# Another written order of issue in a packed attention and gated convolution kernel on one core

## The chip, the core and the metric

One core of a Trainium2 chip runs the whole kernel. TensorE (PE), VectorE (DVE), ScalarE (ACT) and GpSimd (POOL) each take their instructions strictly in the order in which the program lists them; SyncE (SP) only issues the transfers. The metric is the device time in microseconds (us) of one execution; for a kernel it is the median of its runs.

## What is computed

Per batch (8 of them) and head (8 heads, 576 rows, 64 columns), 32 packed queries `p` attend to `k` and `v`; the 576 queries `q` then attend to the 32 packed rows. The heads side by side give `x` (576 x 512), which goes through a causal convolution over 5 rows with a sigmoid, and through two 512 x 512 products:

```python
p_packed = sm_attn(p, k, v)
x = sm_attn(q, p_packed, p_packed)
gate = sigmoid(sum(conv_w[t] * shifted(x, 4 - t) for t in range(5)))
out = (gate * (x @ w_val)) @ w_out
```

The three weights arrive as 64-bit floats and are rebuilt on the chip from their two 32-bit words.

## The kernel before, in words

The work of a batch is cut into pieces, and each kind of piece is a Python generator that issues one piece at every step. A letter names the generator and a digit the batch: `K`, `V`, `Q`, `P` and `L` issue the loads of k, v, q, p and of the weights; `W`, `C` and `O` rebuild w_val, conv_w and w_out; `k` and `q` transpose keys and queries on PE; `a` is the packed attention, `p` transposes its result, `s` and `t` are the second attention's scores and weights, `w` the product of the packed rows with w_val, `x` the second attention's output, `g` the convolution and gate, `v` the value product, `o` the product with w_out and the store. The string `ORDER` (lines 46 to 79) lists the steps one by one; `K0.2` is two steps of `K0`. `run` (line 608) goes through it, and the class `InOrder` (line 82) chains every instruction to the one before it on its engine, so that the string is the order of issue of all five engines. Almost everything has line 90 in the profile for that reason, and groups are told apart by their tiles.

```python
for token in order.split():
    what, n = (token + ".1").split(".")[:2]
    ...
    for _ in range(int(n)):
        next(gens[what])
```

What matters for the steps that follow:

- `load` (line 191) brings a half batch of k, v or q in one transfer, into one of two buffers of its kind (`km`, `vm`, `qm`). `load_p` (185) brings p twice over. `words_of` (208) brings the words of a quarter of w_val in two transfers and of w_out in one, into five buffers.
- `transposed` (302) makes `kpt` or `qpt` on PE (three times 4 transposes a half batch), which ACT copies to `kT` or `qT`. `turned` (324) does the same with p (`pTt`, `pT`) and with the packed result (`ppTt`, `ppT`).
- `attn_pack` (340): scores `s`, their maximum `nb` on DVE, the exponential `a` on ACT, three transposes `at` on PE copied to `a1t` by ACT, the product `pv` with v, scaled to `ppd`.
- `attn_out` (388) and `weighted` (413): scores `s`, a transpose `t` and a maximum `mx` on DVE, a subtraction on POOL, an exponential on ACT, a sum and a reciprocal on DVE, a product on POOL, a transpose `a` on DVE, its rounded and rest parts `a2h` (ACT) and `a2l` (DVE).
- `packed_values` (442): `wp` on PE, split into `wph` (ACT) and `wpl` (DVE). `mixed` (457): `x` on PE, copied to `xp` by ACT. `value` (509): `val` on PE, twelve matmuls; DVE multiplies it into `sig`, ACT and DVE split that into `gvh` and `gvl`. `project` (562): `o` on PE, twelve matmuls for a chunk of 128 rows.
- `gate` (489): ACT starts an accumulator `sig` with the first tap, and DVE adds the other four, each one reading what the one before it wrote.
- `scores`, `packed_values`, `mixed` and the packed product `pv` use parts of PE's array: their matmuls take 64 rows by 32 columns (`s`, `wp`), 32 by 64 (`x`) or a strip of 32 columns (`pv`), several at the same time. They are called tiled here. The transposes, `wo_sum`, `val` and `o` take the whole array.
- The scores, `wp`, `x` and `val` share two PSUM buffers, `big`. A piece that uses `big` therefore waits until the piece two before it in that list has been copied out, by ACT (`x`), by DVE (`val`, the second attention's scores), or by both (`wp`, the first attention's scores). Three buffers `mid` serve the transposes, `pv` and `wo_sum`, and one serves `o`.

Of the kernel before, what the change touches and what calls it, by code (L numbers as in the profile page):

```python
# [45 lines left out]
ORDER = """
x0 L0 K0 L0.3 P0 W0.2 K0 W0 L0 W0 V0 W0 P1 W0 Q0 V0 W0 L0 Q0 W0.7 L0 W0.2 k0 W0 k0.2 P2 W0.2 k0.2 W0 k0.2 L0 C0
W0 K1 k0.2 C0 k0.2 W0 a0 C0 k0.2 W0 a0 k0 W0 K1 C0 a0.2 k1 L0 a0 k1 P3 C0 a0.3 C0 a0.2 q0 a0.2 q0.2 a0.2 q0.2
a0.3 V1 q0 C0 Q1 a0.2 C0 a0.4 O0 V1 a0 p0 O0.2 p0 s0 O0.3 s0.2 O0 s0 q0 O0.2 w0 q0 O0 s0 q0 O0 w0 t0 q0.2 Q1 O0
q0 t0 w0 s0 O0.2 t0 s0 t0 O0 k1 s0 x0 k1 t0 s0 k1 O0.2 x0.2 O0 k1.2 s0 K2 O0 k1.4 t0 a1 x0.2 k1.2 O0 g0 t0 a1 K2  # L50
k1 k2 P4 g0 a1.2 k2 a1 O0.2 a1 t0 O0 a1 g0 a1 t0 q1 x0 O0 a1 q1 t0 a1 O0 q1 v0 g0 a1 q1 x0 O0 g0 x0 O0 g0 q1 O0
g0 a1 v0 Q2 x0 g0 a1.2 q1 O0 q1 a1.2 V2 a1 g0 q1 k2 a1.2 k2 g0 k2 a1.2 k2.2 g0 a1.2 k2 K3 g0 x1 q1 g0 k2 V2 a1
a2 g0 q1 p1 k2 q1 g0 p1 k2 q1 Q2 s1 a2 k2.2 g0 a2 O0 K3 s1 k2 g0 | v0 s1 a2 O0 v0.2 s1 g0 a2 g0 O0 a2 k3 a2.2 g0
s1 q2 P5 s1 k3 v0 a2.2 q2 k3 t1 v0 q2 w1 a2 k3 v0 t1 q2.2 s1 a2 w1 k3 Q3 g0 v0 k3 a2 q2 t1 a2 s1 t1 w1 k3 s1 a2
q2 V3 k3.2 K4 q2 a2 q2 t1 s1 x1 k3 v0 k3 q2 a2 t1 x1.2 k3.2 a2 g0 a2 v0 t1 q2 K4 k3 v0.2 Q3 x1 a2 q2 a2 k4 g0
a2.2 P6 t1 g0 x1 V3 a2 a3 p2 v0 t1 p2 a3 x1 g1 t1 a3 g1 x1.2 v0 g1 w2 v0 x1 o0 g1 w2 g1 w2 g1.2 v1 o0 g1 o0 g1
o0 v1 g1 v1 g1 v1 g1 x2 v1 g1 o0 g1 a3 o0 v1 o0 g1 k4 v1 a3 g1 a3.2 v1 a3 o0 v1 g1 a3 o0 g1 a3 g1 v1 k4 s2 a3 k4
g1 a3 v1 k4 s2 q3 a3 k4 o0 v1 q3 g1 s2 g1 s2 k4 o0 g1 q3 K5 k4 v1 q3 o0 s2 t2 q3 g1 s2 q3 Q4 k4 v1 t2 q3 k4 a3
s2 v1 t2 q3 k4 V4 a3 q3 s2 t2 x2 a3 q3 s2 t2 k4 a3.3 x2.2 a3.2 s2 v1 o1 a3 t2 x2.2 g2 t2 g2 a3 o1.2 q3 t2 a3 a4
q3 g2 Q4 t2 x2 V4 a4 p3 o1 t2 p3 x2 g2 a4 g2.2 x2 g2 s3 o1 g2 k4 x2 o1 q4 s3 k4 k5 K5 v2 q4 g2 P7 s3 a4 g2 s3 q4  # L60
v2 o1 k5 q4 g2 v2 s3 a4 g2 x3 t3 g2 q4 a4 k5 Q5 s3 a4 t3 g2 q4 k5.2 o1 q4 a4 k5 w3 o1 q4 v2 a4 q4 g2 a4 w3 o1 s3
q4 g2 a4 s3 w3 s3 v2 o1 g2 o1 s3 t3 o1 g2 v2 g2 t3 g2 v2 t3 x3 v2 o1 t3 v2 o1 x3 g2 t3 a4 v2 k5 a4 x3 k5 K6 g2
v2 a4 x3 t3 k5 a4 q4 V5 k5 a4.2 v2.2 q4 Q5 a4 t3 g2 t3 g2 x3.2 g3 v2 a4 k5 a4.2 g3 x3.2 k5 g3 k5 a4.2 v2 K6 g3
k5 k6 x3 v2 v3 V5 a4 g3 a5 g3.2 p4 v3 o2 p4 a5 v3 g3 a5 v3 g3 v3 o2 g3 o2 g3 a5 g3 o2 x4 a5 k6 g3 v3 a5.2 g3
v3.2 s4 o2 g3 w4 o2 s4 k6 q5 g3 w4 a5 o2 s4 q5 k6 g3 s4 a5 w4 g3.2 a5 s4 k6 g3 s4 a5 k6 t4 a5 o2 k6 q5 a5 o2 k6
o2 g3 t4 q5 s4 K7 g3 s4 q5 o2 k6 t4 Q6 q5.2 s4 v3 k6 o2 g3 t4 s4 q5 x4 t4 g3 t4 a5 x4 q5 v3 a5 k6 V6 t4 q5.2 k6
a5.2 x4 v3 Q6 t4 a5.2 q5 v3.2 t4 a5 t4 x4.2 a5 g4 v3 x4 a5 g4 a5 v3 x4 g4 x4 V6 a5 a6 v3 p5 x4 g4 k6 p5 o3 k6 a6
K7 g4 a6 g4.2 s5 o3 g4 k7 o3 v4 s5 g4 s5 o3 g4 s5 v4 g4 v4 s5 q6 a6 v4 o3 x5 s5 q6 t5 o3 g4 q6 o3 k7 q6 s5 t5 g4
a6 s5 a6 g4 s5 q6 o3 k7 t5 Q7 q6.2 v4 k7 g4 o3 t5 s5 t5 q6 k7 q6 g4 k7.2 q6 o3 t5 k7 g4 t5 a6 g4 v4 g4 a6 q6 t5
o3 k7 Q7 w5 q6 g4 k7 o3 t5 x5 g4 a6 v4 t5 k7 a6 w5 o3 v4 a6 g4 x5 w5 k7 g4 k7 o3 a6 x5 k7 o3 g4 v4 a6 x5.2 g5 x5  # L70
v4 a6 g5 v4 x5.2 g5 V7 a6.5 g5 x5 v4.2 a6 g5 a6.3 v4 g5.2 V7 v4 g5 a6 a7 p6 v4 v5 p6 g5 a7 o4 v5 a7 g5 v5.2 g5
s6 o4 x6 w6 g5 o4 s6 g5 q7 s6 v5 w6 g5 s6 q7 w6 q7 o4 q7 g5 s6 v5 g5 v5 t6 q7 o4 s6 q7 o4 a7 g5 t6 q7 s6 o4 g5
a7 q7 g5 s6 a7 t6 s6 a7 t6 x6 g5 s6 q7 a7 o4 v5.2 a7 o4 x6 g5 q7 t6 x6 t6 q7 a7 o4 x6 v5 t6 a7 q7 g5 v5 t6 a7 o4
g5 t6 o4 v5.2 x6 g5 t6 x6 a7 g6 v5 a7 g6 x6.2 a7.2 v5 g6 a7.3 v5 v6 x6 a7 g6 o5 g6.3 v6 g6 v6 a7 o5 v6.2 a7 o5
g6 o5 g6.3 x7 g6 v6 a7 o5 g6 v6 o5.2 a7 g6 v6 g6.2 v6 o5 g6 o5 g6 p7 v6 o5 p7 g6 v6 g6 v6 s7 g6 o5 w7 o5 g6 o5
s7 g6 w7 s7.2 w7 v6 s7 o5 t7 o5 s7 v6 t7 s7 v6 t7 v6 o6 t7 s7 x7 o6 t7 s7 o6.2 x7 s7 t7 x7 o6 t7 o6.2 x7.2 t7 g7
t7 g7 t7 x7 o6 g7 v7 o6 x7 g7.2 o6 g7.2 v7 g7 v7 x7 g7 o6 v7.2 o6 x7 g7.2 o7 g7.2 v7 g7 v7 g7 v7.2 o7 g7.4 v7 g7
v7.3 o7 g7.4 o7 v7.3 o7.15
"""


# [570 lines left out]
```

## Time and profile before

| | us |
|---|---|
| median of 3 runs | 317.77 |
| lowest and highest run | 317.33, 321.48 |
| span of the profiled execution | 320.0 |
| first and last matmul of the profile | 16.1, 314.3 |

The profiled execution's span is longer than two of the three times shown, so its own time is the highest of them, 321.48 us, which is 1.5 us around the span and 3.7 us above the median. In the profile a row of the timeline gives the start, the length, the engine, the operation, the output and input tiles and the number of instructions merged into it; matmuls of 32-bit floats are recorded twice each. A length of a matmul goes to its modelled end, so that neighbours overlap, and what a matmul costs in the row of work is the distance from its start to the next start. The rows of the stretches of time give for each engine the busy time and, last, the share of the transfer engines and their GB/s.

### The profile page before, as it was taken

The numbers are of one execution on the slowest core, as the hardware profiler recorded it, in microseconds if no ns is written. First come the engines' busy times: TensorE is split into PE (matmuls) and PEld (weight loads), VectorE is DVE, ScalarE is ACT, GpSimd is POOL, SyncE is SP. The second block draws the span as 40 slices with busy tenths as digits, with TensorE's granted clock in tenths as the row PEclk, the third lists the DMA queues.
The fourth block names the chain that finished last, engine by engine and source line by source line (L and its number), as shares of the span: only waits on it lengthen the run. The fifth ranks groups of instructions, "written<-read, shape, count | busy, mean of one in ns | idle before, by whom it ended". The sixth has DMA issues, their size and how long they took to land.

```text
span 320.0 us, 7365 instructions
## 1 busy us (share of the span) xinstructions
PE 289.8 (91%) x3012; PEld 211.5 (66%) x3012; DVE 260.4 (81%) x404; ACT 209.6 (66%) x424; POOL 50.6 (16%) x59
## 2 busy tenths in 40 slices
PE   0099977998989999999999999999999999999992
PEld 0067434656748876777876867877677788767881
DVE  0773599989998999899989988996899978868761
ACT  2155267988885678677967794887578755556431
POOL 1330122002300041221002312310023000230000
PEclk9999999999999999999999999999999999999999
DMA  7999999599992176941980697262402012111005
GB/s 170 218 223 268 272 231 226 111 229 172 212 221 87 37 175 136 233 126 66 215 191 35 168 209 170 62 160 81 130 33 68 35 33 69 66 66 35 33 2 165
DMA packets 42476, 43.50 MB, mean 136 GB/s; under 512 B 6085, under 2 KB 36805, under 8 KB 42442
## 3 DMA queue, kind: packets, MB, share of 16 engines
q1 hardware_dynamic: 42442, 43.02, 57.3%
q8 instruction: 24, 0.39, 0.6%
q14 instruction: 10, 0.08, 0.1%
HBM read 33.57 MB, written 9.44 MB: 134 GB/s over the span
## 4 chain that ended last, share of the span: by engine, by line
PE 84%; ACT 5%; DVE 4%; DMA 4%; issue 1%; POOL 1%; SPq 0%; ACTq 0%
PE o L90 32%; PE val L90 15%; PE s L90 6%; PE kpt L90 6%; PE qpt L90 5%; PE x L90 5%; PE pv L90 4%; PE at L90 4%; DMA p<-in_p_dram 2%; PE wp L90 2%; PE wo_sum L90 2%; DMA km<-in_k_dram 2%; ACT sig L90 1%; PE ppTt L90 1%; PE pTt L90 1%; DVE wo_words L90 1%
## 5 line engine op out<-in xcount | busy, mean ns | idle before, releaser
L90 DVE SCALAR_TENSOR_TENSOR sig<-xp,cw,sig 128x576 f32<-128x576 f32 x128 | 108.3, 846 | 7.9 <-ACT sig L90 6.7
L90 PE MATMUL o<-woh,gvh 128*128 128x512 f32 x144 | 58.8, 408 | 0.1
L90 PE MATMUL o<-woh,gvl 128*128 128x512 f32 x144 | 56.5, 393 | 0.0
L90 PE MATMUL o<-wol,gvh 128*128 128x512 f32 x144 | 56.4, 391 | 0.0
L90 PE MATMUL val<-a2h,wph 128*128 128x288 f32 x128 | 39.7, 310 | 0.0
L90 PE MATMUL val<-a2h,wpl 128*128 128x288 f32 x128 | 37.9, 296 | 0.0
L90 PE MATMUL val<-a2l,wph 128*128 128x288 f32 x128 | 37.7, 295 | 0.0
L90 POOL TENSOR_TENSOR t<-t,mx 128x576 f32<-128x576 f32 x16 | 22.5, 1404 | 90.6 <-DVE mx L90 89.1
L90 ACT COPY osb<-o 128x512 f32<-128x512 f32 x34 | 19.8, 581 | 24.3 <-PE o L90 19.3
L90 ACT ACTIVATE sig<-sig 128x576 f32<-128x576 f32 x32 | 22.0, 686 | 20.1 <-DVE sig L90 20.0
L90 PEld LDWEIGHTS o<-woh,gvh 128*128 128x128 f32 x144 | 27.0, 188 | 9.0 <-issue 2.2
L90 DVE SCALAR_TENSOR_TENSOR sig<-sig,val 128x576 f32<-128x576 f32 x32 | 23.8, 743 | 11.2 <-ACT sig L90 6.4
L90 PEld LDWEIGHTS o<-woh,gvl 128*128 128x128 f32 x144 | 27.1, 188 | 6.9 <-DVE gvl L90 0.8
L90 PEld LDWEIGHTS o<-wol,gvh 128*128 128x128 f32 x144 | 27.1, 188 | 4.5
L90 ACT CAST gvh<-sig 128x576 fp32r<-128x576 f32 x32 | 21.6, 676 | 11.3 <-DVE sig L90 10.4
L90 POOL TENSOR_TENSOR t<-t,rs 128x576 f32<-128x576 f32 x16 | 20.6, 1288 | 50.1 <-DVE rs L90 42.8
L90 DVE TENSOR_TENSOR gvl<-sig,gvh 128x576 fp32r<-128x576 f32 x32 | 25.3, 792 | 1.6 <-ACT gvh L90 1.4
L90 PE MATMUL qpt<-ident,qm 96*128 96x96 f32 x192 | 25.7, 259 | 0.9 <-DVE sm L90 0.9
L90 PEld LDWEIGHTS qpt<-ident,qm 96*128 96x128 f32 x192 | 19.6, 146 | 9.9 <-issue 5.0
L90 PE MATMUL kpt<-ident,km 96*128 96x96 f32 x192 | 25.9, 267 | 0.0
L90 PEld LDWEIGHTS val<-a2h,wph 128*128 128x128 f32 x128 | 24.1, 189 | 2.5 <-issue 1.8
L90 PEld LDWEIGHTS kpt<-ident,km 96*128 96x128 f32 x192 | 20.1, 151 | 8.3 <-issue 4.2
(78 smaller groups left out, 509.8 us busy)
## 6 DMA issues: line engine op xcount, KB each, us to landing
km<-in_k_dram SPq DMA_DIRECT2D x16, 576.0 KB, 7.3
vm<-in_v_dram SPq DMA_DIRECT2D x16, 576.0 KB, 8.3
qm<-in_q_dram SPq DMA_DIRECT2D x16, 576.0 KB, 7.4
out_dram<-osb SPq DMA_DIRECT2D x24, 256.0 KB, 2.0
wv_words<-in_moe_w_val_dram SPq DMA_DIRECT2D x8, 256.0 KB, 8.0
wo_words<-in_moe_w_out_dram SPq DMA_DIRECT2D x4, 512.0 KB, 11.6
out_dram<-osb SPq DMA_DIRECT2D x8, 192.0 KB, 3.0
p<-in_p_dram SPq DMA_DIRECT2D x16, 64.0 KB, 8.3
```

The lines of the kernel that those rows point to most:

```text
L90: made = getattr(self.engine, op)(*args, **kw)
```

## The change

Only the string `ORDER` is another one; every step is issued as often as before, and no function differs. Cut to the parts spoken of (the string has 32 rows before and 31 after):

```diff
 ORDER = """
-x0 L0 K0 L0.3 P0 W0.2 K0 W0 L0 W0 V0 W0 P1 W0 Q0 V0 W0 L0 Q0 W0.7 L0 W0.2 k0 W0 k0.2 P2 W0.2 k0.2 W0 k0.2 L0 C0
-W0 K1 k0.2 C0 k0.2 W0 a0 C0 k0.2 W0 a0 k0 W0 K1 C0 a0.2 k1 L0 a0 k1 P3 C0 a0.3 C0 a0.2 q0 a0.2 q0.2 a0.2 q0.2
...
+K0.2 L0 P0 W0 k0.3 W0 k0 W0.2 k0 L0 k0 W0 L0 k0.2 W0 k0 a0 W0 k0 a0 k0 a0 k0 Q0 W0.2 L0.2 P1 k0 W0 k0 V0 W0.2 a0 q0 k1
+W0 a0 q0 W0.2 C0 W0 k1 a0 W0 a0.4 V0 W0 a0 C0 W0 a0.4 C0 L0 q0 C0.2 a0.2 q0 C0 a0.2 W0 a0.3 W0 a0 q0 C0 W0.2 a0 K1 p0
...
```

Three places show what the strings make of the engines. SP issues the transfers; the head of its list before (names end in a running number; `km`, `vm`, `qm` are halves of k, v, q, `wv` and `wo` are w_val and w_out):

```order
L90 DMA wv_words<-in_moe_w_val_dram 64x1024 x2
L90 DMA km_0_83<-in_k_dram 96x4x384
L90 DMA wv_words<-in_moe_w_val_dram 64x1024 x6
L90 DMA p_94<-in_p_dram 128x2x64 x2
L90 DMA km_1_100<-in_k_dram 96x4x384
L90 DMA cw_words<-in_moe_conv_w_dram 5x1024
L90 DMA vm_0_106<-in_v_dram 96x4x384
L90 DMA p_109<-in_p_dram 128x2x64 x2
L90 DMA qm_0_113<-in_q_dram 96x12x128
L90 DMA vm_1_115<-in_v_dram 96x4x384
```

and after:

```order
L88 DMA km_0_78<-in_k_dram 96x4x384
L88 DMA km_1_80<-in_k_dram 96x4x384
L88 DMA wv_words<-in_moe_w_val_dram 64x1024 x2
L88 DMA p_85<-in_p_dram 128x2x64 x2
L88 DMA wv_words<-in_moe_w_val_dram 64x1024 x4
L88 DMA qm_0_154<-in_q_dram 96x12x128
L88 DMA wv_words<-in_moe_w_val_dram 64x1024 x2
L88 DMA cw_words<-in_moe_conv_w_dram 5x1024
L88 DMA p_163<-in_p_dram 128x2x64 x2
L88 DMA vm_0_173<-in_v_dram 96x4x384
L88 DMA vm_1_222<-in_v_dram 96x4x384
```

Both halves of k and the first p now stand ahead of three quarters of w_val, and the first half of q ahead of v. The ten or eleven rows move the same transfers in both.

PE from its eighth piece on, at the start of batch 0, before:

```order
L90 MATMUL s_0_1_215<-kT_1_174,pT_139 32x288 x8
L90 MATMUL pTt_224<-ident,p_109 128x128 x2
L90 MATMUL at_0_0_244<-ident,a_0_0_212 96x128 x2
L90 MATMUL at_0_1_249<-ident,a_0_0_212 96x128 x2
L90 MATMUL qpt_0_0_253<-ident,qm_0_113 128x96 x4
L90 MATMUL at_0_2_259<-ident,a_0_0_212 96x128 x2
L90 MATMUL qpt_0_1_263<-ident,qm_0_113 128x96 x4
L90 MATMUL pv_0_269<-vm_0_106,a1t_0_243 32x64 x24
```

and after:

```order
L88 MATMUL s_0_1_177<-kT_1_125,pT_93 32x288 x8
L88 MATMUL qpt_0_0_187<-ident,qm_0_154 128x96 x4
L88 MATMUL pTt_192<-ident,p_163 128x128 x2
L88 MATMUL at_0_0_215<-ident,a_0_0_150 96x128 x2
L88 MATMUL at_0_1_219<-ident,a_0_0_150 96x128 x2
L88 MATMUL at_0_2_229<-ident,a_0_0_150 96x128 x2
L88 MATMUL pv_0_233<-vm_0_173,a1t_0_214 32x64 x24
```

The second p (`pTt`) stands behind the first q transposes and ahead of the three `at`, and one group of q transposes has gone behind `pv`.

PE in batch 2's output `x`, before:

```order
L90 MATMUL qpt_1_1_1510<-ident,qm_1_1099 128x96 x4
L90 MATMUL x_0_0_1517<-a_2_1434,ppd_870 64x288 x4
L90 MATMUL at_1_0_1529<-ident,a_3_1_1306 96x128 x2
L90 MATMUL at_1_1_1533<-ident,a_3_1_1306 96x128 x2
L90 MATMUL x_0_1_1537<-a_2_1434,ppd_870 64x288 x4
L90 MATMUL at_1_2_1543<-ident,a_3_1_1306 96x128 x2
```

and after:

```order
L88 MATMUL at_1_1_1400<-ident,a_3_1_1153 96x128 x2
L88 MATMUL x_0_0_1408<-a_2_1296,ppd_767 64x288 x4
L88 MATMUL x_0_1_1414<-a_2_1296,ppd_767 64x288 x4
L88 MATMUL at_1_2_1421<-ident,a_3_1_1153 96x128 x2
L88 MATMUL kpt_1_1_1424<-ident,km_1_1290 128x96 x4
```

The two halves of `x` now follow each other. That happens at 13 of the 16 pairs of `x` groups, where before it happened at one. Over the whole list PE passes 149 times between a tiled and a whole-array piece or between two kinds of tiling before, and 113 times after. On DVE the taps stand so that 31 instructions on a `sig` accumulator directly follow the one that wrote it, where before 40 did.

More of the change, by code (lines that the diff above doesn't have):

```diff
@@ L46 @@
 ORDER = """
-x0 L0 K0 L0.3 P0 W0.2 K0 W0 L0 W0 V0 W0 P1 W0 Q0 V0 W0 L0 Q0 W0.7 L0 W0.2 k0 W0 k0.2 P2 W0.2 k0.2 W0 k0.2 L0 C0
-W0 K1 k0.2 C0 k0.2 W0 a0 C0 k0.2 W0 a0 k0 W0 K1 C0 a0.2 k1 L0 a0 k1 P3 C0 a0.3 C0 a0.2 q0 a0.2 q0.2 a0.2 q0.2
-a0.3 V1 q0 C0 Q1 a0.2 C0 a0.4 O0 V1 a0 p0 O0.2 p0 s0 O0.3 s0.2 O0 s0 q0 O0.2 w0 q0 O0 s0 q0 O0 w0 t0 q0.2 Q1 O0
-q0 t0 w0 s0 O0.2 t0 s0 t0 O0 k1 s0 x0 k1 t0 s0 k1 O0.2 x0.2 O0 k1.2 s0 K2 O0 k1.4 t0 a1 x0.2 k1.2 O0 g0 t0 a1 K2
-k1 k2 P4 g0 a1.2 k2 a1 O0.2 a1 t0 O0 a1 g0 a1 t0 q1 x0 O0 a1 q1 t0 a1 O0 q1 v0 g0 a1 q1 x0 O0 g0 x0 O0 g0 q1 O0
@@ L52 @@
[L52 to L76, printed above, removed]
@@ L77 @@
-t7 g7 t7 x7 o6 g7 v7 o6 x7 g7.2 o6 g7.2 v7 g7 v7 x7 g7 o6 v7.2 o6 x7 g7.2 o7 g7.2 v7 g7 v7 g7 v7.2 o7 g7.4 v7 g7
-v7.3 o7 g7.4 o7 v7.3 o7.15
+K0.2 L0 P0 W0 k0.3 W0 k0 W0.2 k0 L0 k0 W0 L0 k0.2 W0 k0 a0 W0 k0 a0 k0 a0 k0 Q0 W0.2 L0.2 P1 k0 W0 k0 V0 W0.2 a0 q0 k1
+W0 a0 q0 W0.2 C0 W0 k1 a0 W0 a0.4 V0 W0 a0 C0 W0 a0.4 C0 L0 q0 C0.2 a0.2 q0 C0 a0.2 W0 a0.3 W0 a0 q0 C0 W0.2 a0 K1 p0
+W0 C0 q0 O0 x0 p0 Q0 s0 w0 k1 O0.2 k1.2 K1 s0.2 k1.2 s0 k1 a1 O0.2 s0 w0 q0 t0 q0 L0 O0 t0 q0 O0 w0 q0 a1 Q1 O0 q0.2
+t0 a1 s0 P2 s0.2 k1 x0 O0.2 k1 x0 O0 k1 O0 t0 x0 L0 k1.2 K2 k1 s0 q1 k2 O0 x0 K2 t0 a1 q1 V1 s0 a1 k2 t0 g0 q1 g0 O0
@@ new lines @@
+q1 a1.2 q1 O0.2 q1 x0 O0 k2.2 g0 a1.2 k2.2 a1 k2 O0 a1 t0.2 O0 k2 a1 x0 a1 g0 k2 O0 x0 g0 t0 k2 x0 a2 O0 g0 t0 g0 k2.2
+L0 x0 k2 a2 g0 k2 g0 O0 Q1 O0 V1 a1 a2.2 g0 a1 v0 a1 g0 O0.2 g0.2 a1 a2 x1 a1 q1 a1 P3 O0 K3 a1 g0 q1 a1.2 a2 q1 O0
+a2.2 q1 a2 a1.2 k3.2 v0 g0 a2.2 O0 p1 q1 a2 p1 g0 O0 s1 Q2 s1 a2 w1 s1 q1 w1 k3.2 s1 k3 g0 V2 O0 | q2 v0 k3 s1 q2.2 O0
+w1 g0 v0 K3 t1 O0 v0 Q2 t1 g0 s1 P4 a2 v0 s1 k3 t1 g0 v0.3 a2 q2 k3 V2 q2 v0 s1 g0 t1 q2 k3 a2.2 x1 k3 a2 Q3 x1.2 a2
+a3 v0 g0 a2 x1 a2 k3 K4 a2 P5 t1 s1 a3 k3 v0 s1 g0 a3 k3 v0 t1 k3 q2.2 t1 q2 V3 g0 a3 v0 q2 v0 a3 a2 t1 a3 v0 k4 g1 o0
@@ new lines @@
+a2 g1 x1 p2 k4 t1 g1.2 p2 x1.4 q2.2 a3 k4 P7 a3 k4 g1 a3 s2 t1 a3 g1 k4 s2 a3 q3 g1 s2 v1 o0 k4 g1 a3 q3 v1 q3 a3 g1
+q3 g1 s2 K4 o0 s2 t2 k4.2 w2 g1 s2 V3 a3 w2 a3 w2 a3.2 o0 k4 Q3 t2.2 v1 g1 x2 g1 K5 s2 g1 a3 k4 a3 v1 o0 g1 o0 x2.3 a3
+x2 a3 k4 g2 a3 v1 s2 g1 a4 g2 k4 g1 a3 v1 a3 g2 o0 a4 g1.2 k4 g1 v1 g1 t2 s2 q3 o0 k4 v1 g1 v1 a4 p3.2 v1 Q4 o0 V4 o0
+t2 v1 V4 q3 g2 g1 o0 g1 v1 g2 s2 v1 q3 k5 g2 v1 x2 t2 a4 q3 s3 v1 a4 k5.2 a4 q3 g2 q3 v1 s3 q3 o1 K5 t2.2 k5 t2 k5.2
+q4 s3 x2 q3 x2 g2 x2 t2 x2 o1 g2 s3 k5 v2 q4 g2 v2 k5 a4 k5 s3 g2 v2 k5 q4 g2 v2 a4 s3 w3 o1 q4 w3 a4 q4 g2 P6 s3 o1
@@ new lines @@
+x3 k5 t3 o0 v2 K6 t3 w3 a4 o1 q4 g2 a4 t3 a4 x3 a4 k5 x3 v2 s3 v2 s3 g2 Q4 t3 o1 x3 a4 x3 a5 v2 g2 a4 g3 a5 o1 g2.2 o1
+a4 g3 v2 t3 k5 a4 v2 g3.2 g2 a4 o1 a4 s3 a4 v2 o1 K6 g2 k5 a4 g3 v2 a5 a4 g2 q4 g2.2 g3 k6 t3 x3 a5 q4 a4.2 q4 o1 q4
+k6 g2 a5 g3 o1 a5 t3 v2 k6 p4.2 k6 v2 t3 k6 t3 v2 o1 g3.2 o1 t3 x3.3 q4 a5 Q5 x3 s4 q5 o1 g3 k6 q4 s4 q5 a5 s4.2 v3 k6
+q5 w4 v3 a5 s4 V5 g3 s4 t4 v3 a5 g3 a5 w4 v2 k6 s4 t4 q5 o2 w4 g3 K7 x4 o2.2 g3 a5 v3 k6 a5 t4 Q5 k6 t4 v3 a5 v3 s4 x4
+g3 x4 a5 g3 x4 a5 x4 v3 a5.2 q5 g4 t4 s4 g3 V5 q5 o2 v3 k6 a5 s4 g4 t4 a5.2 g3 o2 k6 a5 v3 g4 g3 t4 v3 o2 v3 a6 g3 g4
@@ new lines @@
+Q6 a5.2 k6.2 a6.2 o2 p5 q5 v3 g3 p5 g4 k7 a6 o2 t4 g3 g4.2 V6 o2 s5 q5 a6 g3 q5 t4 s5 o2 g4 k7 a6 s5 g4 x4 q5 o2 x4.3
+q5.2 g4 q6 Q7 a6 v3 q6 t4 a6 g4 s5 x4 g3 k7 v3 v4 a6 s5 t5 o2 a6 v4 q6 V6 s5.2 v3 q6 v3 k7 g4 o3 k7 g4 a6.2 t5 x5 a6
+k7 g4 t5 g4 x5 g4 o3 x5 v4 s5 t5 K7 x5 a6 w5 q6 t5 a6 g4 s5 a6 w5 v4 o3 s5 a6 g4 a6 x5 t5 o3 g4 v4 a6 q6 o3 w5 a6 t5
+g5 v4 g4 v4 g5 v4 g5 t5 g4 g5 k7 a6.2 v4 g4 t5 Q6 k7 g5 o3 g4 o3 a6 o3 v4 x5.2 g5.2 k7 o3.2 t5 a6 k7 p6 v4.2 q6 g4 v5
+p6 x5 k7 v4 k7 g5.2 v5 q6 g5 k7 x5 o3 v4 k7 s6 g5 s6 x5 o3 g5 s6 g5 q6 q7 a7 q7 a7 g5 v4 s6 x6 a7 s6 a7 q6 a7 o3 a7.2
@@ new lines @@
+q7 v5 g5 t6 a7.2 o3 v5 q6 q7 v4 V7 q6 v5.2 g5 a7 g5 q7 v5 a7 o3 s6 g5 t6 v5 g5 Q7 s6 t6 w6.2 q7 o4 v5 V7 o4 t6 w6 a7.2
+s6 v5 g5 q7 s6 g5 o4 v5 o4 a7 v5 x6 o4 s6 a7 g5 q7 t6 x6.2 a7.2 o4 a7.2 t6 a7 x6 t6 g5 a7 t6 a7 g6 v5 x6 o4 g5 o4 a7
+g6 t6 g6 a7 x6.2 v5 g6 v5 g6.2 v5 x6 o4 t6 p7 g6 o4 p7 x6 o4 g6.3 s7 v6 g6 s7 v6 s7 o4 q7 g6 o5 v6 g6 q7 v6.2 q7 o5
+g6.2 w7 v6 s7.2 t7 q7 w7 t7 s7 g6 w7 g6 s7 x7 o5 v6 o5 t7 g6 o5 g6 v6.2 o5 g6 o5 v6 s7 x7 g6 t7 g6 o5 t7 o5 g6 x7 s7.2
+x7.2 t7 v6 o5 g6 o5 g7 t7 x7 t7 v6 o5 g7 t7 v6.3 g7.2 o5 v6 o5 x7 t7 x7 g7.3 x7 o6 o5 v7 g7 o6 v7 o6 v7 g7 o6 x7 o6 g7
@@ L79 @@
+v7 g7.3 v7 g7 v7 o6.2 v7 o6.2 g7.4 v7 g7 v7 o6 g7 o6 g7 v7.3 g7.2 v7 o7.2 g7 v7.2 o7.2 v7 o7.2 o6 o7.13
 """
```

## The prediction

> **What bounds the kernel now.** I read the busy times first, then the stretches of time, then PE's waits, and last its timeline. The page's busy times and four stretches (start to end, length, then PE, PEld, DVE, ACT and POOL busy) say where to look.
>
> ```profile
> PE 289.8 (91%) x3012; PEld 211.5 (66%) x3012; DVE 260.4 (81%) x404; ACT 209.6 (66%) x424; POOL 50.6 (16%) x59
> ```
>
> ```profile
> 0.00:10.00 10.00, 0.00 (x0) 0.00 (x0) 2.16 (x4) 1.94 (x2) 0.80 (x8) 1.00 0.80 180
> 10.00:20.00 10.00, 3.89 (x22) 3.56 (x22) 7.39 (x12) 4.16 (x9) 4.06 (x3) 1.00 1.10 221
> 20.00:30.00 10.00, 9.42 (x108) 6.01 (x107) 5.64 (x13) 5.55 (x16) 1.28 (x1) 1.00 1.17 238
> 39.00:55.00 16.00, 12.40 (x127) 5.74 (x126) 14.84 (x28) 12.16 (x25) 3.96 (x4) 1.00 1.15 233
> 55.00:92.00 37.00, 34.29 (x513) 23.79 (x515) 33.92 (x56) 32.48 (x74) 5.52 (x6) 1.00 0.90 188
> 92.00:286.00 194.00, 193.23 (x2024) 145.76 (x2020) 171.25 (x261) 136.86 (x274) 32.74 (x35) 1.00 0.45 112
> ```
>
> There are three regimes. Up to 30 us the transfer engines are full (last but one number about 1.1) and PE starts late. From 39 to 92 us PE idles 3.6 + 2.7 = 6.3 us while DVE is busy 48.8 of 53 us: PE and DVE wait for each other. From 92 to 286 us PE idles 0.8 of 194 us, so there only fewer or shorter steps of PE's work gain anything; DVE has 12% to spare.
>
> The start is one wait, the longest of PE, and the chain that ended last begins with the transfers behind it.
>
> ```profile
> PE pTt L90 <- DMA p<-in_p_dram: 16.1, 1, 16.1
> ```
>
> ```profile
> 8.22 7.75 DMA p<-in_p_dram
> ```
>
> PE's timeline of the first 47 us shows the second loss.
>
> ```profile
> 16.11 0.66 PE L90 MATMUL pTt<-ident,p 128*128 128x128 f32 x2 [16.11 <-DMA p<-in_p_dram]
> 16.56 3.54 PE L90 MATMUL kpt<-ident,km 96*128 96x96 f32 x20
> 20.06 1.22 PE L90 MATMUL s<-kT,pT 64*32 64x288 f32 x16
> ...
> 22.68 1.21 PE L90 MATMUL s<-kT,pT 64*32 64x288 f32 x16 [0.57 <-ACT kT L90]
> ...
> 27.24 1.51 PE L90 MATMUL pv<-vm,a1t 96*32 96x64 f32 x48
> ...
> 31.48 1.51 PE L90 MATMUL pv<-vm,a1t 96*32 96x64 f32 x48
> ...
> 34.42 1.22 PE L90 MATMUL s<-qT,ppT 64*32 64x288 f32 x16 [0.47 <-ACT ppT L90]
> 35.56 2.07 PE L90 MATMUL wo_sum<-wo_top,ident 128*128 128x512 f32 x2
> 37.43 1.63 PE L90 MATMUL wo_sum<-wo_words,ident 128*128 128x512 f32 x2
> ...
> 42.95 0.72 PE L90 MATMUL s<-qT,ppT 64*32 64x288 f32 x16 [1.73 <-ACT qT L90]
> ...
> 46.16 0.71 PE L90 MATMUL x<-a,ppd 32*64 32x288 f32 x8
> ```
>
> The same group of scores takes 1.22 us up to 34.42 and 0.72 at 42.95: PE works at about half speed until some time within `wo_sum`, although the granted clock (third number from the end in the stretches) reads 1.00 throughout.
>
> **Part 1, the loads.** Sizes are in this list of transfers (number, KB each).
>
> ```profile
> km<-in_k_dram SPq DMA_DIRECT2D x16, 576.0 KB, 7.3
> vm<-in_v_dram SPq DMA_DIRECT2D x16, 576.0 KB, 8.3
> qm<-in_q_dram SPq DMA_DIRECT2D x16, 576.0 KB, 7.4
> ...
> wv_words<-in_moe_w_val_dram SPq DMA_DIRECT2D x8, 256.0 KB, 8.0
> ...
> p<-in_p_dram SPq DMA_DIRECT2D x16, 64.0 KB, 8.3
> ```
>
> Before, p ends a list of 2 x 256 + 576 + 6 x 256 + 2 x 64 = 2752 KB, 2818 thousand bytes. At the rates of the stretches (180, then 221 GB/s) 3119 thousand had moved when p landed at 15.97 us; the 301 thousand over are later transfers under way at the same time. After, p ends a list of 576 + 576 + 512 + 128 = 1792 KB: 1835 + 301 = 2136 thousand, which 1800 by 10 us and 221 GB/s beyond give 11.5 us. PE starts 4.6 us earlier. The next arrivals by the same sum (238 GB/s after 20 us, the 20 KB of conv_w left out): first half of q, 3392 KB, 18.9 us; second p, 4032 KB, 21.8; first half of v, 4608 KB, 24.2; second half, 5184 KB, 26.7. As both lists contain the same eleven rows of transfers up to there, nothing behind them comes earlier, and v's first half, which stood ahead of the first q, comes later.
>
> So I walk PE through its new list. 11.5: `pTt`, four `kpt` groups at 3.54 / 5 = 0.71 us; 14.8: `s`; then two `kpt`, and the second `s`, which came 2.6 us after the first and now has the exponential of the first ahead of its `kT` copies on ACT, so about 3.0: 17.8 to 19.0. The q transposes then wait for nothing much (18.9). `pTt` of the second p stands at the head of PE's list until 21.8, and the three `at`, `pv` and all that follows stand behind it. They end at 24.0, `pv` waits for v (24.2), ends at 25.7; one `qpt` and three `at` fill 2.3 us, a copy 0.6; the second `pv` at 28.7 instead of 31.48. `qpt`, `cwps` and `ppTt` are behind it on PE, and a `wo_top` on ACT is ahead of `ppT`: the scores `s<-qT` start at 33.0 instead of 34.42. The lead of 4.6 us has become **1.4 us**. Bounds: 0 if ACT's list holds the copies by another 1.4 us; 4.6 if none of it is lost.
>
> **Part 2, from there to 92 us.** The first `x` came 11.7 us behind those scores. It hangs on the chain of DVE, POOL and ACT through `t` and `a`, and on DVE the step `wol`, which needs `wo_sum`, still stands just ahead of `a`. The new list has `wp`, three `kpt`, a score group and one `qpt` ahead of `wo_sum`, so I leave 11.7 us as it is: about 44.8. After that PE has more work that needs no DVE (transposes of batch 2) ahead of the first `val`, which should remove part of the 6.3 us of idle time, but DVE has the same work to do and is nearly full. Of the taps, 9 fewer follow the one whose result they read.
>
> ```profile
> 58.37 0.81 DVE L90 SCALAR_TENSOR_TENSOR sig<-xp,cw,sig 128x576 f32<-128x576 f32 x1
> 59.10 0.69 DVE L90 SCALAR_TENSOR_TENSOR wo_top<-wo_top,wo_words 128x512 uint32<-128x512 uint32 x1
> ```
>
> ```profile
> 62.42 2.50 DVE L90 SCALAR_TENSOR_TENSOR sig<-xp,cw,sig 128x576 f32<-128x576 f32 x3
> ```
>
> A tap followed by another tile's instruction gives way after 59.10 - 58.37 = 0.73 us; three in a chain take (2.50 - 0.81) / 2 = 0.85 each. So 9 x 0.12 = 1.1 us of DVE time, hidden after 92 us behind a PE that doesn't idle, and of use only here. I take **1.0 us** for this part, between a loss of 1.5 (the chain of Part 1's end grows) and a gain of 4.
>
> **Part 3, tiled groups side by side.** A lone group, with a whole-array neighbour on both sides, and then two in a row:
>
> ```profile
> 102.39 0.72 PE L90 MATMUL s<-kT,pT 64*32 64x288 f32 x16
> 103.03 0.50 PE L90 MATMUL o<-woh,gvh 128*128 128x512 f32 x1
> 103.37 0.40 PE L90 MATMUL o<-wol,gvh 128*128 128x512 f32 x1
> 103.60 0.39 PE L90 MATMUL o<-woh,gvl 128*128 128x512 f32 x1
> ```
>
> ```profile
> 199.88 0.49 PE L90 MATMUL qpt<-ident,qm 96*128 96x96 f32 x4
> 200.31 0.71 PE L90 MATMUL s<-kT,pT 64*32 64x288 f32 x16
> 200.82 0.69 PE L90 MATMUL s<-qT,ppT 64*32 64x288 f32 x16
> 201.44 0.55 PE L90 MATMUL qpt<-ident,qm 96*128 96x96 f32 x4
> 201.77 0.47 PE L90 MATMUL o<-woh,gvh 128*128 128x512 f32 x1
> ```
>
> From its start to the next start a lone group of scores takes 0.64 us, the first of two 0.51: 0.13. The `qpt` ahead of a tiled group takes 0.43 against 0.33 of the one behind it: 0.10. The first `o` behind a tiled group takes 0.34 against 0.23: up to 0.11. Taking one lone group away from between whole-array pieces saves two passages and 0.23 to 0.34 us, so about 0.14 us a passage. PE's list has 149 passages before and 113 after: 36 x 0.14 = **5.0 us**, most of it after 92 us where PE is the bound. Bounds: 36 x 0.07 = 2.5 if only the smaller half of these gaps is saved for each, 36 x 0.17 = 6.1.
>
> **Part 4, what it adds.** Two `x` groups in a row ask for both `big` buffers within 0.6 us, so the second waits for the piece before the first. Counting along PE's list with the durations above, at 26 places less than 1 us is left over after the release of `big` without any queue, against 13 before (release by DVE lasts as long as this):
>
> ```profile
> L90 DVE SCALAR_TENSOR_TENSOR sig<-sig,val 128x576 f32<-128x576 f32 x32 | 23.8, 743 | 11.2 <-ACT sig L90 6.4 <-PE val L90 3.5 <-PE ppTt L90 1.3
> ```
>
> All of PE is queued behind the waiting group. The 13 old places cost at most the 0.8 us of idle time after 92 us. For 13 new ones I take 0.15 us each, **2.0 us** lost; bounds 0 and 13 x 0.74 = 9.6, when DVE is one whole instruction late at each. The end of the list (stores, last copies) is the same kind of work: 0.
>
> **Sum.** -1.4 - 1.0 - 5.0 + 2.0 = -5.4 us. The profiled execution took 321.5 us (span 320.0), so it would take 316.1. The median of the runs shown is 3.7 us lower than that execution: 317.8 - 5.4 = **312.4 us**, 1.7% less, with a range of its own of 308.5 to 316.
>
> **The rivals.** *The early start is kept* and the new waits are nil: 317.8 - 4.6 - 1.0 - 5.0 = 307.2 us. For it: PE has no other wait for a transfer later. Against it: the arrivals above.
>
> *PE comes to full speed early.* If it did some 3.5 us after 11.5, the pieces between the arrivals would halve: second `pv` at 27.0, `s<-qT` at about 30 instead of 33.0, and 309.4 us. Against it: before, PE was busy from 16.11 to 34 us with gaps under 0.6 us and stayed slow. The Trainium skill, "TensorE: Matmul & The Clock Gate", Part 1, states that about 3.4 us of sustained work lift the clock to its full rate, and its Part 4 that transposes don't count as such work; the rows at 20.06 and 34.42 speak against the first alone and fit the second.
>
> *The waits for `big` take back what Part 3 gives*: 13 x 0.5 = 6.5 in place of 2.0, and no gain in Part 2: 317.9 us, no change.
>
> *Slower*: the pairs make PE and DVE run in step. At each of the 26 places PE waits a whole DVE instruction of 0.74 us, 19.2 us, less the 7.4 us of the gains: 329.6 us. It decides against the change from 7.4 / 26 = 0.28 us a place, and by more than 2% from 0.53 us. For it: DVE is busy 88% of the time after 92 us and takes its list in order. Against it: `x` is copied by ACT, which has a third of its time free.
>
> *That the change doesn't do what it says* holds for the taps: 31 instead of 40 in a chain is little; it is in Part 2.
>
> **How the numbers follow.** Forecast 0.50, early start kept 0.17, early full speed 0.05, waits take it back 0.18, slower 0.10. Two per cent, about what a measurement of this kernel can tell from no change, lies at 311.4 and 324.1 us. The forecast's own range puts 0.2 of its 0.50 under 311.4 and 0.3 above. Faster: 0.20 + 0.17 + 0.05 = 0.42. Slower: 0.10. Same: 0.30 + 0.18 = 0.48. The range takes in half of the early start and the waits that take it back: 305 to 319.5 us.
>
> **What would show it.** PE's first matmul at 11 to 12 us, its second wait at the second `pTt` until about 22, `s<-qT` of batch 0 at about 33 and the first `x` at 44 to 45.5 show Part 1. PE's idle time between 39 and 92 us slightly under 6.3 shows Part 2. `x` groups 0.5 us apart with 0.64 to the next piece show Part 3, and idle time of PE after 92 us of 2 to 4 us, named as waits of `x`, `s` or `wp` for DVE or ACT, Part 4. The prediction is wrong if the scores `s<-qT` start before 31, if pairs of `x` cost PE as much as two lone ones, or if PE idles over 6 us after 92.

## The result and the profile after

The changed kernel took 309.70 us (median of 4 runs, 309.14 to 314.08) against 317.77 (4 runs, 317.33 to 321.48): 0.971 of the time before, 95% interval 0.964 to 0.979. The ratio is one of means and leaves out the slow run of 314.08 us, so it isn't the quotient of the two medians (0.975). A second set on another occasion gave 313.45 us (6 runs, 309.49 to 316.38) and 0.983 (0.978 to 0.988): less of a gain, and not clear of 2%. The forecast was 312.4, with a range of 305 to 319.5. The times of one kernel lie 4 us and more apart from run to run, and the profile of before that the prediction read is of one of the longer runs; so a second profile of before, of a run of 316.74 us, stands beside it from here on.

The changed kernel's profiled execution took 309.92 us, 307.8 of them the span. Its busy time of PE:

```profile
PE 279.8 (91%) x3012; PEld 211.9 (69%) x3012; DVE 260.9 (85%) x404; ACT 207.9 (68%) x424; POOL 51.2 (17%) x59
```

The stretches of time that were shown of before (length, then PE, PEld, DVE, ACT and POOL busy; the granted clock is third from the end):

```profile
39.00:55.00 16.00, 13.97 (x144) 7.53 (x143) 15.76 (x28) 14.74 (x34) 2.98 (x4) 1.00 1.08 239
55.00:92.00 37.00, 35.64 (x519) 25.60 (x518) 35.45 (x60) 31.68 (x73) 6.10 (x7) 1.00 0.93 190
92.00:286.00 194.00, 192.46 (x2017) 150.47 (x2016) 180.52 (x270) 139.28 (x275) 33.85 (x36) 1.00 0.45 116
```

PE idles 2.0 + 1.4 = 3.4 us from 39 to 92 us (6.3 before) and 1.5 us from 92 to 286 (0.8 before). Its waits name small amounts (total, number, longest):

```profile
PE pTt L88 <- DMA p<-in_p_dram: 14.3, 2, 11.7
PE s L88 <- ACT kT L88: 2.2, 2, 1.4
...
PE wp L88 <- DVE sig L88: 0.7, 1, 0.7
...
PE s L88 <- DVE sig L88: 0.5, 2, 0.3
```

And the head of PE's timeline:

```profile
11.69 0.66 PE L88 MATMUL pTt<-ident,p 128*128 128x128 f32 x2 [11.69 <-DMA p<-in_p_dram]
...
18.58 0.72 PE L88 MATMUL s<-kT,pT 64*32 64x288 f32 x16 [1.42 <-ACT kT L88]
19.30 0.52 PE L88 MATMUL qpt<-ident,qm 96*128 96x96 f32 x4
22.39 0.66 PE L88 MATMUL pTt<-ident,p 128*128 128x128 f32 x2 [2.57 <-DMA p<-in_p_dram]
...
28.55 1.51 PE L88 MATMUL pv<-vm,a1t 96*32 96x64 f32 x48
...
32.06 0.72 PE L88 MATMUL s<-qT,ppT 64*32 64x288 f32 x16 [0.70 <-ACT ppT L88]
...
41.07 0.71 PE L88 MATMUL x<-a,ppd 32*64 32x288 f32 x8
```

The arrivals are those of the prediction (11.7 for 11.5, second p at 22.4 for 21.8, second `pv` at 28.55 for 28.7). Not foreseen is the `s` at 18.58: it takes 0.72 us, PE is at full speed by then, and at 28.55 `pv` takes 1.51 us, half speed again, where the later 0.88 would be full. The first `x` is at 41.07, not at 44.8.

### The profile page after: what moved, and what is told of

Read it like the earlier page. It is cut to its first block, busy times and chain, and to the rows that moved or that the text cites. A ratio compares the mean times of both kernels' runs of the same rounds, so it can differ in the third digit from the quotient of the medians.

```text
span 307.8 us, 7341 instructions
## 1 busy us (share of the span) xinstructions
PE 279.8 (91%) x3012; PEld 211.9 (69%) x3012; DVE 260.9 (85%) x404; ACT 207.9 (68%) x424; POOL 51.2 (17%) x59
## 4 chain that ended last, share of the span: by engine, by line
PE 52%; DVE 32%; DMA 8%; ACT 4%; issue 2%; POOL 1%; ACTq 0%; POOLq 0%; DVEq 0%
PE o L88 23%; DVE sig L88 15%; PE val L88 10%; PE x L88 3%; DMA vm<-in_v_dram 3%; DMA wv_words<-in_moe_w_val_dram 3%; PE pv L88 3%; PE qpt L88 3%; DVE gvl L88 3%; DVE sm L88 3%; PE s L88 2%; PE kpt L88 2%; PE at L88 2%; DVE t L88 2%; PE wp L88 2%
## 5 line engine op out<-in xcount | busy, mean ns | idle before, releaser
L88 PE MATMUL o<-woh,gvh 128*128 128x512 f32 x144 | 58.7, 408 | 0.3 <-ACT osb L88 0.3
L88 POOL TENSOR_TENSOR t<-t,mx 128x576 f32<-128x576 f32 x16 | 23.2, 1450 | 86.4 <-DVE mx L88 86.4
L88 DVE TENSOR_TENSOR gvl<-sig,gvh 128x576 fp32r<-128x576 f32 x32 | 26.9, 843 | 3.9 <-ACT gvh L88 3.9
L88 ACT COPY kT<-kpt 128x384 f32<-128x384 f32 x48 | 22.8, 483 | 5.3 <-PE kpt L88 5.1
L88 PE MATMUL kpt<-ident,km 96*128 96x96 f32 x192 | 24.6, 262 | 0.7 <-DVE wol L88 0.5
```

Of the source, the lines that this page charges most:

```text
L88: made = getattr(self.engine, op)(*args, **kw)
```

## The experiments

**The two kernels again, unchanged.** A second profile of each shows what belongs to the kernel and what to the run.

> The kernel before, unchanged, for a profile of one of its usual runs (its times cluster at about 317.5 and at about 321.8 us, and the first profile is of 321.5). Theory (the moment at which PE's clock comes up sets which of the two it is): 317.5 us, with the first matmul at 16.1 as before, PE at full speed from about 27 us instead of 38, the scores s<-qT of batch 0 at about 31.7 instead of 34.42, the first x at about 41.8 instead of 46.16, and everything behind it about 4 us earlier. Rival (the 4 us lie elsewhere, in transfers or late in the kernel): rows up to 50 us within 0.5 us of those of the first profile.

It took 316.74 us, span 314.6. PE in the second profile of before:

```profile
15.59 0.66 PE L90 MATMUL pTt<-ident,p 128*128 128x128 f32 x2 [15.59 <-DMA p<-in_p_dram]
...
30.17 0.72 PE L90 MATMUL s<-qT,ppT 64*32 64x288 f32 x16 [0.47 <-ACT ppT L90]
...
36.74 0.85 PE L90 MATMUL s<-qT,ppT 64*32 64x288 f32 x16 [1.74 <-ACT qT L90]
37.52 2.08 PE L90 MATMUL wo_sum<-wo_top,ident 128*128 128x512 f32 x2
...
41.30 0.71 PE L90 MATMUL x<-a,ppd 32*64 32x288 f32 x8
```

The first `x` comes 46.16 - 41.30 = 4.9 us earlier than in the first profile, and the execution is 321.5 - 316.7 = 4.8 us shorter: all of the difference between the two runs lies ahead of the first `x`. PE came up to full speed at about 20 us here, and at about 38 in the first profile. The theory holds, with an even earlier rise than it named.

> The changed kernel as it is, beside the others on the same chip: 309 to 311 us by its first measurement (309.1 to 314.1). If the runs spread by 4 us and more, the speed of PE in the first 40 us should differ between two profiles of the same program, and little else.

Median 313.45 us; its profile (span 308.5) has the rows of the changed kernel's first one up to the first `x` within 0.5 us: `s<-qT` at 31.8, first `x` at 40.8, half speed from 20 to 30 us. Both profiles of the changed kernel are of short runs (309.92 and 310.59 us), so what its runs of 313 to 316 us do differently isn't seen.

**Pairs of tiled groups, undone.** In the changed string, a step that uses the whole array is put back between the two `x` groups at 10 of the 13 pairs; PE's list has 132 passages instead of 113. The first of them:

```diff
-x1 k3 a2 Q3 x1.2 a2
+x1 k3 a2 Q3 x1 a2 x1
```

> The changed kernel with one whole-array piece put back between the two x groups at 10 of its 13 adjacent pairs; 132 passages instead of 113. Theory of the passage: 19 x 0.14 = 2.7 us more, 312.4 us. Rival (adjacent pairs cost as much in waits as they save): 309.7 us, no difference.

315.41 us (12 runs, 312.17 to 319.49), 0.990 of before (0.987 to 0.994). The median is 5.7 us above the changed kernel's in its first set and 2.0 above that in its second; the lowest run is 3.0 us above its lowest. So the times alone don't give the price, and the rows do. One place in both, `x` twice, a q transpose and one `at`; first the changed kernel, then with the pair apart:

```profile
163.13 1.20 PE L88 MATMUL x<-a,ppd 32*64 32x288 f32 x16
164.26 0.42 PE L88 MATMUL at<-ident,a 128*96 128x128 f32 x2
164.52 0.50 PE L88 MATMUL qpt<-ident,qm 96*128 96x96 f32 x4
164.80 0.48 PE L88 MATMUL o<-woh,gvh 128*128 128x512 f32 x1
```

```profile
168.58 0.71 PE L88 MATMUL x<-a,ppd 32*64 32x288 f32 x8
169.22 0.55 PE L88 MATMUL qpt<-ident,qm 96*128 96x96 f32 x4
169.70 0.71 PE L88 MATMUL x<-a,ppd 32*64 32x288 f32 x8
170.34 0.42 PE L88 MATMUL at<-ident,a 128*96 128x128 f32 x2
170.53 0.48 PE L88 MATMUL o<-woh,gvh 128*128 128x512 f32 x1
```

The same four pieces take 164.80 - 163.13 = 1.67 us with the pair and 170.53 - 168.58 = 1.95 with it apart: 0.28 us for two passages, 0.14 each, as the prediction had it. From the first `o` on neither profile has a stretch at half speed, and PE idles 1.5 us in both. From there to the start of the last matmul the changed kernel takes 302.11 - 83.44 = 218.67 us, and the one with pairs undone 308.69 - 87.14 = 221.55: 2.9 us for 18 of the 19 passages, 0.16 each. (The whole profiled execution is longer by more, since PE was also at half speed from 31.1 to 34.5 and from 51.6 to 58.4 us in it.)

**Pairs alone.** In the string before, the first `x` group of each pair and its copy are moved to just ahead of the second, at all 16; 125 passages instead of 149, all else as before. Two of the places:

```diff
-s0 t0 O0 k1 s0 x0 k1 t0 s0 k1 O0.2 x0.2 O0
+s0 t0 O0 k1 s0 k1 t0 s0 k1 O0.2 x0.3 O0
...
-q1 x0 O0 a1 q1 t0 a1 O0 q1 v0 g0 a1 q1 x0 O0 g0 x0 O0
+q1 O0 a1 q1 t0 a1 O0 q1 v0 g0 a1 q1 O0 g0 x0.3 O0
```

> The kernel before, with only the first x group of each half batch moved down to its second one, so that all 16 pairs are adjacent; 125 passages between ways of using the array instead of 149. Theory of the passage (0.14 us each): 24 x 0.14 = 3.4 us less, 314.4 us, and PE's rows of adjacent x groups 0.5 us apart. Rival (PE waits for the PSUM pair big as long as it saves): 317 to 319 us, with PE waits of x for DVE or ACT of 2 us or more after 92 us.

324.86 us (323.9 to 329.16), 1.022 of before (1.020 to 1.024): slower than either expectation, although 24 passages at 0.14 us should save 3.4. The stretch after 92 us, and two of PE's waits (totals of the whole profile):

```profile
92.00:286.00 194.00, 188.20 (x1977) 144.72 (x1977) 168.63 (x256) 133.89 (x269) 32.62 (x34) 1.00 0.43 109
```

```profile
PE o L88 <- ACT osb L88: 1.9, 3, 0.8
...
PE x L88 <- ACT xp L88: 1.5, 2, 0.8
```

PE idles 5.8 us where it idled 0.8, nearly all of it in waits named as waits for copies by ACT, in whose list the copies of `x` now stand elsewhere: 1.0 us of `pv` for `a1t`, 0.9 of `ppTt` for `ppd`, 0.8 of `x` for the copy of the group before it (`xp`, the other `x` wait is earlier), and smaller ones. Waits for the release of `big`, which Part 4 of the prediction feared, are among them. By the estimate of the next section 3 to 4 us more are lost ahead of that stretch, between the first `x` and the first `o`, where PE was also at half speed from 47.6 to 51.0 us. The pairs pay only in a list in which the other steps are placed to cover these waits; the changed list is such a one, the old list with pairs put in is not.

**Early loads alone.** In the string before, the two loads of k, the first words of w_val and the first p go to the front:

```diff
-x0 L0 K0 L0.3 P0 W0.2 K0 W0 L0 W0
+K0.2 L0 P0 x0 L0.3 W0.3 L0 W0
```

> The kernel before, with only the head of the list of loads changed: both halves of k, the first quarter of w_val and the first p, then all else as before. First theory (the early start is lost again at the transfers that come later): PE's first matmul at 11.5 us, but about 1.5 us left at the second scores, 316 us. Rival (PE keeps the lead, because nothing else waits for a transfer): 317.8 - 4.6 = 313 us. Third (what counts is when PE's clock comes up, which does not depend on the loads): 317 to 318 us.

321.83 us (321.25 to 326.25), 1.013 of before (1.011 to 1.016). PE starts at 11.1 us, and then waits; PE's waits and ACT's timeline:

```profile
PE kpt L88 <- ACT pT L88: 4.2, 1, 4.2
PE s L88 <- ACT kT L88: 3.1, 3, 1.7
PE kpt L88 <- ACT kT L88: 2.4, 1, 2.4
```

```profile
11.69 0.66 ACT L88 ACTIVATE wv_top<-wv_words 128x512 f32<-128x512 f32 x1
13.44 0.68 ACT L88 ACTIVATE wv_top<-wv_words 128x512 f32<-128x512 f32 x1 [1.08 <-DMA wv_words<-in_moe_w_val_dram]
16.24 0.68 ACT L88 ACTIVATE wv_top<-wv_words 128x512 f32<-128x512 f32 x1 [2.12 <-POOL wv L88]
16.81 0.38 ACT L88 ACTIVATE pT<-pTt 128x256 f32<-128x256 f32 x1
```

The copy `pT` stands behind three conversions of w_val on ACT, and these have become later, since the words of w_val now come behind k: the first starts at 11.69 us instead of 7.04, the third, which waits for POOL's work on the first, at 16.24 instead of 13.01. `s<-qT` starts at 35.25 us, against 30.17 in the second profile of before. Early data was of no use here without ACT's list changed with it, as the changed string does.

**The changed list with its loads as before.** The first twelve load steps stand in the old order, all others as changed:

```diff
-K0.2 L0 P0 W0 k0.3 W0 k0 W0.2 k0 L0 k0 W0 L0 ...
+L0 K0 L0.3 P0 K0 L0 V0 P1 Q0 V0 W0 k0.3 W0 k0 ...
```

> The changed kernel with the first twelve steps of its list of loads in the order of the kernel before; everything else as changed. If the early k and p carry the gain of the first 90 us: PE starts at 16 us and the time is 309.7 + 4.5 = 314 us or more. If they are worth only what is left at the second scores (1.4 to 2.4 us): 311 to 312 us. If the order of the pieces after that carries it: 310 us.

317.31 us (12 runs, 315.33 to 320.91), 0.998 of before (0.994 to 1.002). First matmul at 16.1 us, first `x` at 46.6, 5.5 later than in the changed kernel; behind it nothing differs by more than 0.3 us. By its time the first expectation came nearest. The loads and the rest of the head belong together: with the old loads the changed list loses ahead of the first `x` what it saves behind it. How much of the 5.5 is the transfers' own can't be said, since PE was at half speed from 23.4 to 33.6 and from 37.0 to 40.4 us in this run.

**Taps in a chain.** Three of the four DVE taps of each chunk are moved to just ahead of the last one, so that 99 of them follow the one they read instead of 31:

```diff
-o0 k4 g1 a3 q3 v1 q3 a3 g1 q3 g1 s2 K4 o0 s2 t2 k4.2 w2 g1 s2 V3
+o0 k4 a3 q3 v1 q3 a3 q3 s2 K4 o0 s2 t2 k4.2 w2 g1.4 s2 V3
```

> The changed kernel with the four taps of every chunk on DVE in one row, so that 99 instead of 31 instructions on a sig accumulator directly follow the one that wrote it. That is 68 x 0.12 = 8 us of DVE time. If DVE time beyond 92 us is hidden behind PE, as the prediction has it: 309.7 + about 1 = 311 us. If DVE has become a second bound (it is busy 94% of the stretch from 92 to 275 us in the changed kernel): 314 to 318 us.

340.37 us (339.52 to 342.32), 1.072 of before (1.069 to 1.076); neither expectation came near. DVE is busy 269.7 us instead of 260.9: 8.8 us for 68 taps, 0.13 each, close to the 0.12 of the prediction. Most of the loss comes from elsewhere:

```profile
92.00:286.00 194.00, 177.38 (x1916) 134.55 (x1915) 166.43 (x245) 129.04 (x264) 28.61 (x33) 0.97 0.44 109
```

```profile
PE s L86 <- DVE sig L86: 4.4, 2, 3.7
```

PE idles 16.6 us in this stretch (1.5 in the changed kernel), and the granted clock (0.97) shows half speed in between. The longest wait, of scores for the release of a buffer by DVE, lasts 3.7 us, about a block of four taps (4 x 0.85) with the product behind it; the rest of the idle time lies in many smaller waits for DVE and ACT. So it isn't the sum of DVE's time alone that counts, but also how many instructions stand in a row ahead of a release: DVE had 7% to spare after 92 us in the changed kernel, and one block still stopped PE for 3.7 us. The spans differ by 32.6 us. 27.2 of them lie behind the first `o`: 17.4 more of idle time and 13.7 us at half speed, which cost up to 6.8; about 3 stay unexplained. 3.3 lie ahead of the first `x`, where no tap stands and PE was at half speed until 40.5 us instead of 30.3, so the order of the taps isn't their cause; the other 2 or so lie between the first `x` and the first `o`.

**PE kept busy.** Extra matmuls of the identity by itself, which nobody reads, so that the computation stays the same. All of them are made by the function below. The first kernel is the one before with 100 at the head of PE's list; the second the changed one with 80 there and 24 at its wait for the second p; the third the one before with 56; the fourth the changed one with 36 and 10; the fifth the changed one with only the 10 at the wait. The first one's edit (at the wait the call stands in a step `D0` of the order, between `q0` and `k1` of its first row):

```diff
+    def warm(n):
+        ps = one("warm", "out")
+        for _ in range(n):
+            pe.matmul(ps[:, :P], ident, ident, start=True, stop=True)
+
+    warm(100)
```

> The kernel before with 100 matmuls on the identity ahead of its first transpose, into the PSUM buffer that the output product uses later; PE would else be idle then. They add nothing to what is computed. If PE's half speed up to about 38 us sets the pace of the first stage: PE's score groups take 0.72 instead of 1.22 us from 20 us on, the scores s<-qT start 3 us or more earlier, and the time is 311 to 314 us. If the transfers and the lists of ACT and DVE set it: 317 to 318 us.

> The changed kernel with 80 such matmuls ahead of its first transpose and 24 more ahead of the second p's transposes, where PE waits 2.6 us. If PE's speed sets the pace there: pieces from 15 to 30 us in half the time, the scores s<-qT at 30 us or before instead of 32.1, 306 to 308 us, and less spread between runs. If the transfers set it: 309 to 311 us.

Both were sized wrongly: 100 took 24 us, so PE's own work began at 25.4 us in the one (326.25 us, 1.026, 1.023 to 1.030) and at 21.1 in the other (321.97, 1.014, 1.010 to 1.018). As times they tell little. As rows they tell what full speed is worth: in the kernel before, from its first own matmul to `s<-qT`, PE took 39.06 - 25.36 = 13.7 us at full speed throughout, against 34.42 - 16.11 = 18.3 in the first profile and 30.17 - 15.59 = 14.6 in the second. (The data had long landed by then, too; in the second profile the longest wait for a transfer in that stretch is 0.64 us.)

> The kernel before, with 56 extra matmuls of the identity by itself at the head of PE's list; they write a PSUM tile that nobody reads, end before the first p lands (16.1 us) and add nothing to what is computed. Theory (PE's half clock up to 27 or 38 us costs the head of the kernel): full speed from about 16 us on, s<-qT of batch 0 at 30 us or earlier, 314 to 316 us (0.985 to 0.995 of before), and the spread of 4 us between runs gone or smaller. Rival (the head is set by arrivals and by ACT's list, PE's speed hardly matters): 317 to 318 us, s<-qT at 31.5 or later.

321.78 us (320.96 to 322.60), 1.015 of before (1.012 to 1.018), over the median of before in every run: as to the time both expectations failed, and rows of the last section show what happened; only the spread is smaller, 1.6 us. The extra work ends at 16 us as meant and PE is at full speed there. It then waits 2.36 us for the second half of k, a wait that the slower PE of the first profile doesn't have; from 22.2 to 39.3 it is at half speed, and `s<-qT` starts at 34.98.

> The changed kernel with 36 such extra matmuls at the head of PE's list (they end before p lands at 11.7) and 10 more between the last q transposes and the second pTt, where PE waits 2.6 us for p. Theory (clock): full speed throughout from about 12 us, s<-qT of batch 0 at about 30.3 instead of 32.1, 307 to 309 us with a smaller spread than the 309 to 316 of the changed kernel. Rival (arrivals and ACT's list set the head): 309 to 314 us as the changed kernel, s<-qT at 31.5 or later.

311.47 us (309.06 to 313.65), 0.983 (0.977 to 0.989). Half speed from 17.4 to 24.2 us, `s<-qT` at 32.17: no gain. The 10 matmuls at the wait ran at half speed, 0.43 us each, so 4.3 us for a wait of 2.6.

> The changed kernel with only the 10 extra matmuls at the 2.6 us wait for the second p. Theory (it is this wait that puts PE back to half speed from 20 to 30 us): the granted clock stays up through 20 to 30 us, s<-qT of batch 0 at about 30.5, 308 to 310 us, spread smaller. Rival (the clock falls back for another reason, or its fall costs nothing): the clock reads 0.50 from 20 to 30 us again, or s<-qT stays at 31.5 to 32 us, and 309 to 316 us.

313.73 us (310.54 to 315.98), 0.987 (0.982 to 0.991). PE came up only at 24.6 us in the profile, so that the fall at 20 us which the fill was to prevent could not show, and the run doesn't test the theory. The changed kernel's own profile speaks against it: by the windows of the last section 1.67 us are idle in the window ahead of the fall at 20.06, and 1.42 of them are the second `s` waiting for `kT`, while the wait for p begins only at 19.82. The 10 matmuls took 4.3 us here too, `s<-qT` came at 32.24, and the profiled execution (313.98 us) has a stretch at half speed later, from 51.9 to 58.7. The fill brought no gain and the spread stayed.

## Why the prediction was right, and where it was not

To compare lists of another order I add up along PE's list what each piece costs at full speed by its shape and its neighbours (0.64 and 0.51 us for a lone group of scores and the first of two, and so on): 270.6 us before, 265.3 after. A piece's start less the sum ahead of it is what has been lost by then, to waits and to half speed. These sums are estimates: with another choice of the typical cost among the rows the two sums lie 5.0 to 7.3 us apart, so a part below may be off by about 1 us.

| us lost up to | first `x` | first `o` | last piece |
|---|---|---|---|
| before, first profile | 32.0 | 41.4 | 43.2 |
| before, second profile | 27.2 | 36.3 | 38.1 |
| changed | 26.3 | 34.6 | 37.3 |
| changed, pairs undone (sum 268.3) | 27.3 | 38.2 | 40.8 |

Against the second profile the spans differ by 314.6 - 307.8 = 6.8 us: 0.9 by the first `x`, 0.8 from there to the first `o`, 5.3 by the sums, 0.7 behind the last piece's start, less 0.9 lost more between the first `o` and the last piece.

**Part 3, the passages (-5.0):** right. 36 fewer, 5.3 us by the sums, and undoing 18 of them where nothing else differs cost 2.9. It is the bulk of the gain, and the only part that the experiments separate cleanly.

**Part 4, the new waits (+2.0):** the mechanism is there, the size was 0.9. PE's idle time after 92 us rose from 0.8 to 1.5 us, not to the 2 to 4 that were named as its sign; 1.2 of it are waits of `wp` and `s` for `sig` on DVE, which no profile of before has there. Where the other steps aren't placed for it, the loss is much larger (pairs alone). The rival of a slower kernel (329.6 us) comes near the time of that list, 324.86, but the waits there are for ACT, not for DVE as it had it.

**Part 2, up to the first `o` (-1.0):** 0.8 against the second profile, 1.1 against the first. PE's idle time from 39 to 92 us fell to 3.4, not to slightly under 6.3, since before it is 4.3 in the second profile (with the stretch at half speed in it).

**Part 1, the loads (-1.4):** the arrivals and the loss of the lead to the second `pTt` were right. The step that failed is "The first `x` came 11.7 us behind those scores ... so I leave 11.7 us as it is": it came 9.0 us behind. The prediction let this `x` hang on the chain through DVE, POOL and ACT. The tile `a` that `x` reads was written sooner than that, here in the first and second profile of before and in the changed kernel:

```profile
44.58 0.77 DVE L90 STREAM_TRANSPOSE a<-t 128x576 f32<-128x576 f32 x1
```

```profile
38.36 0.77 DVE L90 STREAM_TRANSPOSE a<-t 128x576 f32<-128x576 f32 x1
```

```profile
40.10 0.77 DVE L88 STREAM_TRANSPOSE a<-t 128x576 f32<-128x576 f32 x1
```

It ends at 45.35 and 39.13 us, 0.8 and 2.2 us ahead of `x`, and only in the changed kernel (40.87) just ahead of it. So before the change PE's own list set the first `x`. In the list before, the second `s<-qT` and two pairs of `wo_sum` stand between, and in both profiles of before one pair of `wo_sum` runs at half speed there; in the new list one pair has gone behind the first `x`, with a group of scores and three `kpt` in its place, and the other runs at full speed. The kernel before with 100 extra matmuls, at full speed all the way, has the first `x` 48.83 - 39.06 = 9.8 us behind the scores. So of 11.7 - 9.0 = 2.7 us that the prediction missed, about 2.0 are PE's half speed in the first profile and 0.8 the new order. Against the first profile the first `x` gained 5.1 us, against the second 0.2 (0.9 with the work ahead of it counted), so the forecast's size fits the second run and its working fits neither. The error under it is that the prediction took PE's half speed for a property of the head of this kernel, while it is one of the run: the first profile has it until 38 us, the second until 20.

**Early full speed, the rival at 309.4:** its time is near the measured 309.7, its mechanism isn't what happened. PE did reach full speed 5 us after its start, then lost it from 20.1 to 30.3, and `s<-qT` started at 32.06, not at 30. The "early start kept" (307.2) isn't what happened either: PE waits 2.57 us at the second `pTt`, as Part 1 had it.

**The sum:** the term of 3.7 us between the profiled execution and the median was right to be kept apart; the second profile shows that it lies wholly ahead of the first `x`. 316.7 - 5.4 = 311.3 for a run like the second profile's, 309.9 measured.

## What to carry to other kernels

Count the passages between tiled and whole-array pieces in a PE that is never idle: 0.14 to 0.16 us each here, and they can be saved by order alone, provided that the copies which release the buffers are placed for it. Before a profile's head is costed, look whether PE runs at full speed in it, and take a second profile if runs differ: in this kernel some 1.5 us of waiting within 3.4 us were mostly followed by 3.4 to 20 us at half speed. An edit that helps in a list that was arranged as a whole can hurt when it is put alone into another list.
